# Two row transfers as one step of a planner, and a new rank table: a spectral filter and an MLP mixed by a gate, on one Trainium2 core

## The chip, the core and the metric

The kernel runs on one core of a Trainium2 chip. The core has TensorE (PE in the profile; its weight loads are PEld), VectorE (DVE), ScalarE (ACT), GpSimd (POOL), SyncE (SP, which here only issues transfers) and 16 DMA engines. Each engine works through its own instructions in the order in which the program holds them, and waits on semaphores for the others. The metric is the device time of one execution in microseconds (us), as the median of several runs; lower is better.

## The reference, cut to what matters

```python
def _A_ref(x, w_r, w_i):                      # x: 1 x 2048 x 512
    X = jnp.fft.rfft2(x, axes=(-2, -1))
    X = X * (w_r + 1j * w_i)                  # 2048 x 257
    return jnp.fft.irfft2(X, s=(S, D), axes=(-2, -1))

def _B_ref(x, w1, b1, w2, b2):
    h = jnp.einsum("bsd,df->bsf", x, w1) + b1   # F = 1792
    h = _gelu(h)
    return jnp.einsum("bsf,fd->bsd", h, w2) + b2

g = _sigmoid((x * gate_w).sum(-1, keepdims=True))
return g * a + (1 - g) * b                    # a = _A_ref, b = _B_ref, both of x
```

All data is float32. The output has 2048 x 512 elements.

## The kernel before, in words

**Arithmetic.** The MLP runs as matmuls on numbers that are split in a high part (rounded to 12 bits) and a low part: a product is three matmuls, high by high, high by low and low by high. Splitting costs one copy on ACT (the high part, names ending in h) and one subtraction on DVE (the low part, ending in l). The 2048 rows of x are four column blocks c of 512. F is 14 blocks f of 128. For blocks c = 0 and 1 (`mlp`, three passes over f) an up-projection is 12 matmuls into `ph`, then Gelu on ACT, then the split into `g_f h` and `g_f l` (L557, L558), then the down-projection in groups of three matmuls into `po`; ACT empties `po` into `o` (L1066, L1069) and a transfer adds it into `bacc` in HBM. Blocks 2 and 3 (`fast`, four passes) use a scheme with seven products for eight (`nu`, `ux`) and `poB`, `oB`.

**The spectral half.** The 2048 positions are 128 x 16. `forward(j)`, for 16 values of j, does the transform along the features (`pd`) and over 128 positions (`py`) by matmul and leaves the result in `y[j]`, a slice of one tile `yy` of 128 partitions; partition p below 64 holds the frequency p, partition 64 + p the frequency -p (partition 64: -64), each with real and imaginary part side by side. The transform over the remaining 16 values of j is two stages of four-point butterflies on DVE: `stage1` (tiles a0 to a3) and the first part of `filt` (b0 to b3), then the product with the filter (`wf` times `y` into `m`, L852, sums L854 and L856) and the way back: c0 to c3, `stage4` (d0 to d3) and `inverse` by matmul (`pz`, `pa`).

**The two special rows.** The frequencies p and -p are made as sum and difference of two rows; frequencies 0 and 64 have no such partner, so what rows 0 and 64 of `yy` get in this way is not their spectrum. `own_rows` (L738) computes these two rows by itself: eight small transfers (L732) gather them from all `y[j]` into a tile `own` of 64 partitions, one matmul with the constant `fx` does the 16-point transform (`pown`, L742), ACT copies the result to `ownr` (L744), and two transfers write it back, 32 partitions of `ownr` each into one partition of `yy` (L746). They overwrite what `stage1` left in those rows, so they come after all of `stage1`, and they come ahead of every instruction of `filt`, which reads whole tiles.

**The order.** Nothing is issued where it is written. The code makes 2017 steps; a step (`Graph.add`, L267) has an engine, a cost, a lag until its result is there, a function that emits its instructions, and the buffers that it reads and writes. From the buffers the graph takes what a step must wait for: the last writer of what it reads, and the last writer and all readers of what it writes. `schedule` (L309) then plays the steps through by their costs: whenever an engine is free it takes, among the steps whose predecessors are done and for which buffer slots are free, the one with the lowest rank (L326). For a transfer on SP a step is done at the end of its time on the wire plus its lag (L385), and only then do its successors become free. What comes out is one list of all steps, and the program is emitted in that order. The ranks come from the table `RANKS` (L128), one number for each step in the order of their making, times 0.05 (L1320). The numbers run from 0 to 2015 and come close to the step's place in the list.

So two things differ: in the planner the second transfer of L746 has the first as its predecessor (both write all of `Y`) and starts when that has landed by the planner's costs; in the emitted program each is an instruction of SP that waits for what it really depends on, and SP issues in the list's order.

What the steps are called that stand around these transfers:

- `gt` (L1285): four transfers that spread the gate's values over the partitions; `wf` (L843): one filter slice each; `wb9l_raw`, `wa11l_raw` and so on (L964): weights; `bacc<-o` (L1067): a down-projection's result to HBM.
- `g_8l`, `g_9l`, `g_5l` ... (L558): low parts of the hidden values for the down-projection, on DVE; the up-projection's accumulator `ph` is free only when the low part has been made.
- the product on `wf` with `rev` (L847): a few elements of a filter slice, on DVE.
- `b0d` (L754) and `b0s` (L752): the first two differences and sums of `filt(0)`.
- `xf`, `xft`, `tt`, `xb`: differences of x that `spread_x` (L1105) makes for blocks 2 and 3.

Of the kernel before, what the change touches and what calls it, by code (L numbers as in the profile page):

```python
# [37 lines left out]
HP = P // 2  # L38
# [394 lines left out]
def tile_kernel(ctx: ExitStack, tc: tile.TileContext, xt, xc, w1, w2, b1, b2, x0g, wf, wrev, out, consts):  # L433
# [10 lines left out]
    vec, act, pe, sp = nc.vector, nc.scalar, nc.tensor, nc.sync  # L444
# [9 lines left out]
    add = g.add  # L454
# [283 lines left out]
    def own_rows():  # L738
# [6 lines left out]
        for k in range(2):  # L745
            add("sp", 0.2, 2.6, lambda k=k: sp.dma_start(yy.ap()[k * HP:k * HP + 1], r.ap()[k * R // 2:(k + 1) * R // 2, 0]), [r], Y)  # L746
# [627 lines left out]
```

## Time and profile before

| | us |
|---|---|
| median of 3 runs | 368.69 (367.57 to 368.77) |
| the profiled execution's own time | 368.5 |
| its span, first to last instruction | 366.7 |
| PE busy in the span | 359.2 |
| DVE busy | 329.1 |
| ACT busy | 255.6 |
| POOL busy | 69.5 |

The span is 1.8 us shorter than the execution's own time: that is what lies around the instructions. The granted clock of TensorE is 0.999 over the whole span. A row of the profile's tables names a line, an engine, an operation and the tiles (out<-in, without numbers of buffers); "q" behind an engine is its issuing of transfers, which isn't counted as busy. Times of matmuls are modelled at their ends, and they overlap: a matmul of 512 columns is shown with 0.39 us and the next one starts 0.23 us after it.

### The profile page before, as it was taken

To read this page: it belongs to the slowest core of one execution; us is meant where nothing else is said; L and a number is where in the kernel's file an instruction comes from. 1 tells how busy PE (TensorE), PEld (TensorE's weight loads), DVE (VectorE), ACT (ScalarE), POOL (GpSimd) and SP (SyncE) were. 2 spreads that over 40 slices of the span, in tenths; PEclk is the share of its full clock that TensorE was granted. 3 is DMA by queue.
4 is the path that set the end of the run, shared out by engine and by line. 5 is a ranking of instruction groups with operands and counts; after the bars stand their busy time and mean duration, and the time that the engine had idled before them with its cause. 6 is when DMAs were issued, how large, how long until landed. Compare 5 with 4: busy or idle time off the path is not lost.

```text
span 366.7 us, 5738 instructions
## 1 busy us (share of the span) xinstructions
PE 359.2 (98%) x1808; PEld 302.8 (83%) x1808; DVE 329.1 (90%) x746; ACT 255.6 (70%) x471; POOL 69.5 (19%) x89
## 2 busy tenths in 40 slices
PE   8999999999999999999899999999999999999996
PEld 8888888898788778887688888888888788888885
DVE  5899989999838899999999999999999868989982
ACT  5976788788977222653758876999999997755300
POOL 0210001100204111220333200001241212112210
PEclk9999999999999999999999999999999999999999
DMA  7999785458787936999998954148788637899787
GB/s 250 284 336 309 240 250 132 88 170 252 185 196 133 215 39 123 314 203 337 210 236 200 209 133 117 57 150 207 118 146 170 94 53 157 171 296 230 190 254 217
DMA packets 46719, 70.35 MB, mean 192 GB/s; under 512 B 5600, under 2 KB 19424, under 8 KB 46688
## 3 DMA queue, kind: packets, MB, share of 16 engines
q1 hardware_dynamic: 34880, 48.93, 40.7%
q0 software_dynamic: 11376, 20.71, 35.5%
q8 instruction: 14, 0.23, 0.3%
q10 hardware_dynamic: 432, 0.33, 0.3%
q14 instruction: 17, 0.14, 0.1%
HBM read 48.32 MB, written 19.41 MB: 185 GB/s over the span
## 4 chain that ended last, share of the span: by engine, by line
PE 76%; DVE 12%; DMA 5%; ACT 3%; issue 2%; SPq 1%; DVEq 0%; ACTq 0%
PE poB L507 20%; PE po L507 13%; PE ph L507 12%; PE ux L1181 10%; PE nu L1181 8%; PE pz L507 4%; PE pd L507 3%; PE py L507 3%; PE pa L507 3%; DMA y<-ownr 2%; DVE m L852 2%; DMA wf<-in_wf 1%; DMA rev<-in_wrev 1%; DVE y L752 1%; DMA xf<-in_x0g 1%
## 5 line engine op out<-in xcount | busy, mean ns | idle before, releaser
L991 ACT ACTIVATE ph<-ph,b1t 128x512 f32<-128x512 f32 x28 | 18.4, 656 | 19.4 <-PE ph L507 19.3
L498 POOL DMA_DIRECT2D bacc<-o x16 | 14.3, 893 | 51.2 <-ACT o L1069 49.2
L890 ACT ACTIVATE sw<-y,al 64x512 f32<-64x512 f32 x32 | 22.5, 719 | 0.5
L498 POOL DMA_DIRECT2D bacc<-oB x16 | 14.3, 933 | 41.8 <-ACT oB L1069 41.6
L852 DVE TENSOR_TENSOR m<-y,wf 128x514 f32<-128x514 f32 x32 | 20.8, 690 | 0.0
L1069 ACT ACTIVATE o<-po 128x512 f32<-128x512 f32 x16 | 9.5, 595 | 15.8 <-PE po L507 15.8
L507 PE MATMUL pd<-cf,w 128*128 128x129 f32 x128 | 18.2, 275 | 0.2 <-DVE cf L622 0.2
L507 PEld LDWEIGHTS pz<-tg,pq 128*128 128x128 f32 x128 | 16.9, 191 | 1.5 <-ACT od L931 0.4
L507 PEld LDWEIGHTS pd<-cf,w 128*128 128x128 f32 x128 | 16.8, 190 | 1.3 <-DVE cf L622 0.4
L507 PE MATMUL pz<-tg,pq 128*128 128x128 f32 x128 | 17.4, 275 | 0.0
L1181 PE MATMUL nu<-xf,wa0h 128*128 128x512 f32 x56 | 17.4, 391 | 0.0
L507 PE MATMUL py<-zb,tf 128*128 128x258 f32 x96 | 17.2, 295 | 0.0
L897 DVE SCALAR_TENSOR_TENSOR pq<-y,al,sw 128x256 f32<-128x256 f32 x32 | 15.0, 480 | 0.7 <-ACT sw L893 0.7
L507 PEld LDWEIGHTS py<-zb,tf 128*128 128x128 f32 x96 | 14.1, 189 | 1.1 <-ACT pys L716 0.2
L507 PEld LDWEIGHTS pa<-zb,ci 128*128 128x128 f32 x96 | 13.8, 188 | 1.4
L507 PE MATMUL pa<-zb,ci 128*128 128x256 f32 x96 | 14.6, 283 | 0.0
L698 DVE TENSOR_TENSOR zb<-pd,zb 128x256 fp32r<-128x256 f32 x32 | 13.1, 418 | 0.9 <-ACT zb L695 0.7
L723 ACT ACTIVATE y<-pys 64x257 f32<-64x257 f32 x32 | 12.9, 416 | 1.3 <-DVE pys L720 0.8
L665 DVE TENSOR_TENSOR w<-eo 128x256 f32<-128x256 f32 x32 | 12.8, 418 | 0.0
L662 DVE TENSOR_TENSOR eo<-xf 128x256 f32<-128x256 f32 x32 | 12.6, 419 | 0.0
L910 DVE TENSOR_TENSOR zb<-pz,zb 128x512 fp32r<-128x512 f32 x16 | 11.0, 687 | 1.3 <-ACT zb L909 1.2
L1181 PEld LDWEIGHTS nu<-xf,wa0h 128*128 128x128 f32 x56 | 10.4, 188 | 2.1
(701 smaller groups left out, 1274.1 us busy)
## 6 DMA issues: line engine op xcount, KB each, us to landing
wf<-in_wf SPq DMA_DIRECT2D x16, 257.0 KB, 5.1
bacc<-o POOLq DMA_DIRECT2D x16, 256.0 KB, 5.9
bacc<-oB POOLq DMA_DIRECT2D x16, 256.0 KB, 4.5
xf<-in_xt SPq DMA_DIRECT2D x14, 256.0 KB, 5.2
wr<-in_w SPq DMA_DIRECT2D x14, 256.0 KB, 5.6
tf<-tf SPq DMA_DIRECT2D x16, 192.0 KB, 3.2
bacc<-o SPq DMA_DIRECT2D x8, 256.0 KB, 3.6
ba<-bacc SPq DMA_DIRECT2D x8, 256.0 KB, 4.5
```

The costliest lines, as they stand in the source:

```text
L498: return add("pool", 2.3 * kb / 340, 3.4, lambda: nc.gpsimd.dma_start(dst(), src(), accum_op=ALU.add), reads, writes, rank)
L507: pe.matmul(ps, w, x, start=start, stop=stop)
L662: v(lambda s=s, op=op: vec.tensor_tensor(eo.ap()[:, s], x.ap()[:, 0:2], x.ap()[:, 2:4], op=op), 256, [x], [(eo, s)], feed)
L665: v(lambda s=s, op=op: vec.tensor_tensor(w.ap()[:, s], eo.ap()[:, :, 0], eo.ap()[:, :, 1], op=op), 256, [eo], [(w, s)], feed)
L698: v(lambda c=c: vec.tensor_tensor(segs(xl, c), both(c), segs(xh, c), op=ALU.subtract), 256, [ps[c], (xh, c)], [(xl, c)], 0)
L723: a(lambda o=o, i=i: act.activation(Y[j].ap()[o:o + HP, 1], pys.ap()[i:i + HP, 1], AF.Copy), 257, [(pys, 1)], [(Y[j], 1 + k)], 0, more=0.1)
L852: v(lambda mk=mk, k=k, y=y, w=w: vec.tensor_tensor(mk.ap(), y.ap(), w.ap()[:, k:k + 1, :ND].to_broadcast([P, 2, ND]), op=ALU.mult), 514, [ ...
L890: a(lambda sw=sw, y=y, o=o, i=i: act.activation(sw.ap()[o:o + HP], y.ap()[i:i + HP, ::-1, :HD], AF.Copy, scale=al.ap()[i:i + HP, 0:1]), 51 ...
L897: v(lambda sw=sw, pq_=pq_, y=y, j=j, k=k, op=op: vec.scalar_tensor_tensor(pq_.ap()[:, k], y.ap()[:, k, :HD], al.ap()[:, 1 + j:2 + j], sw.a ...
L910: v(lambda n=n, ps=ps: vec.tensor_tensor(zl.ap()[:, :, :, n], ps.ap(), zh.ap()[:, :, :, n], op=ALU.subtract), 512, [ps, (zh, n)], [(zl, n) ...
L991: a(lambda: act.activation(ps.ap(), ps.ap(), AF.Gelu_apprx_tanh, bias=b1t.ap()[:, f:f + 1]), 600, [b1t], [ps]).table = "gelu"
L1181: pe.matmul(o.ap(), w(wi, e), FX[j].ap()[:, xi, e], start=first, stop=k == 5, skip_group_check=not start)
```

## The change

The two transfers of `own_rows` become one step that issues both; its cost is 0.4 instead of twice 0.2, its lag 3.0 instead of 2.6. There are 2016 steps then. The table of ranks is another one. Both kernels issue the same transfers and compute the same. The description of the change also says that a reader of one tile row no longer holds up the other's writer; no other line differs.

```diff
 RANKS = """
-11 19 10 20 28 24 44 42 36 41 34 7 14 0 13 16 21 4 43 32 12 8 5 3 6 9 120 60 74 83 85 39 52 67 96 17 22 26 95 97 109
...
+0 12 294 321 326 399 330 333 323 340 343 1 13 7 14 20 23 11 35 26 10 2 5 8 19 4 32 56 47 53 78 22 42 73 43 45 21 25 72
...
@@ -742,8 +742,12 @@
         add("pe", c_pe4(ND), 0.25, lambda: mm(ps.ap()[:, :ND], t.ap(), own.ap()[:, :ND], True, True), [t, own], [ps], 0)
         r = t2k("ownr", cls="own")
         a(lambda: act.activation(r.ap()[:R, 0], ps.ap()[:, :ND], AF.Copy), 257, [ps], [r], 0)
-        for k in range(2):
-            add("sp", 0.2, 2.6, lambda k=k: sp.dma_start(yy.ap()[k * HP:k * HP + 1], r.ap()[k * R // 2:(k + 1) * R // 2, 0]), [r], Y)
+
+        def back():
+            for k in range(2):
+                sp.dma_start(yy.ap()[k * HP:k * HP + 1], r.ap()[k * R // 2:(k + 1) * R // 2, 0])
+
+        add("sp", 0.4, 3.0, back, [r], Y)
```

The table holds one number for each step and can't be read as it stands. These are the ranks, old and new, of the steps around the transfers, found by counting the steps in the order of their making:

| step | engine | old rank | new rank |
|---|---|---|---|
| `bacc<-o` of block 1, last quarter | SP | 708 | 678 |
| `wb9l_raw` | SP | 711 | 693 |
| third `gt` | SP | 701 | 705 |
| `wf` of k2 = 8 | SP | 702 | 708 |
| `pown` | PE | 697 | 701 |
| `ownr` | ACT | 704 | 709 |
| last two differences of `stage1(3)` | DVE | 692, 696 | 702, 706 |
| the two row transfers | SP | 706, 719 | 712 (one step) |
| fourth `gt` | SP | 715 | 716 |
| `g_8l`, `g_9l` of block 0 | DVE | 710, 718 | 710, 722 |
| product on `wf` of k2 = 8 | DVE | 720 | 725 |
| first `b0d` | DVE | 734 | 726 |
| `g_5l` of block 1 | DVE | 725 | 730 |
| up-projections f = 5, 6, 7 of block 1 | PE | 713, 722, 730 | 714, 741, 732 |
| `sw3`, first half | ACT | 1422 | 1538 |
| first `d0s` | DVE | 1606 | 1532 |

154 rows, old and new, of the table RANKS are left out of this document.

## The prediction

> **What bounds the kernel now.** First the page's span and its row of busy times, to see which engine is full.
>
> ```profile
> span 366.7 us, 5738 instructions
> PE 359.2 (98%) x1808; PEld 302.8 (83%) x1808; DVE 329.1 (90%) x746; ACT 255.6 (70%) x471; POOL 69.5 (19%) x89
> ```
>
> TensorE (PE) is busy for 359.2 of 366.7 us, so nearly everything that can be won is time in which PE does not get its next matmul. Where that is, the view by stretches of time tells. Its columns are the stretch, its length, then busy us and instructions of PE, its weight loads, DVE, ACT and POOL, the granted clock, the share of the DMA engines and GB/s.
>
> ```profile
> 0.00:100.00 100.00, 98.25 (x552) 85.62 (x552) 89.77 (x243) 78.70 (x167) 11.88 (x23) 1.00 0.78 228
> 100.00:111.00 11.00, 11.00 (x49) 8.79 (x49) 4.08 (x9) 9.10 (x15) 1.72 (x2) 1.00 0.86 208
> 111.00:190.00 79.00, 77.39 (x336) 62.40 (x335) 76.71 (x162) 38.14 (x68) 20.13 (x23) 1.00 0.85 199
> 190.00:240.00 50.00, 50.00 (x222) 41.32 (x222) 48.92 (x101) 41.45 (x75) 7.86 (x9) 1.00 0.61 147
> 240.00:300.00 60.00, 59.48 (x308) 50.06 (x307) 56.15 (x118) 58.58 (x102) 14.91 (x18) 1.00 0.69 136
> 300.00:360.00 60.00, 60.00 (x325) 51.81 (x324) 51.80 (x112) 29.66 (x50) 12.99 (x15) 1.00 0.85 211
> 360.00:366.70 6.70, 3.08 (x25) 2.84 (x24) 1.66 (x5) 0.00 (x0) 0.00 (x0) 0.92 0.65 207
> ```
>
> From 111 to 190 us PE is idle for 1.6 us and DVE is at 76.71 of 79.00 us (97%). The matmuls overlap in their records, so the idle time understates the loss; the counts tell it. From 190 to 240 us PE has no idle time and runs 222 matmuls, one each 0.227 us (222 x 0.227 = 50.3 us, the last one hanging over the edge). At that pace the 336 of the stretch before need 76.2 us; with the same overhang that stretch had room for 79.3. So **PE loses about 3.1 us between 111 and 190 us**, and that is the largest loss inside the run (0 to 100 us: 1.75 us idle, 240 to 300 us: 0.52; the end, 3.6 us, is the last output's way home).
>
> Why DVE is late there, the chain of waits shows (start, length, what):
>
> ```profile
> 104.17 6.69 DMA y<-ownr
> 110.95 1.30 DVE b0d L754 x2
> ...
> 181.51 0.61 DVE g_12l L558
> 182.16 1.90 PE po L507 x7
> ```
>
> The chain runs from the second of the two row transfers (y<-ownr) into the first addition of the filter's first group (b0d) and through DVE to 182 us, where it passes to PE. DVE itself, in order of time:
>
> ```profile
> 101.20 0.69 DVE L754 TENSOR_TENSOR y<-a3s,a3s 128x514 f32<-128x514 f32 x1
> 102.79 0.69 DVE L558 TENSOR_TENSOR g_8l<-ph,g_8h 128x512 fp32r<-128x512 f32 x1 [0.91 <-ACT g_8h L557]
> 105.67 0.69 DVE L558 TENSOR_TENSOR g_9l<-ph,g_9h 128x512 fp32r<-128x512 f32 x1 [2.19 <-ACT g_9h L557]
> 106.28 0.16 DVE L847 SCALAR_TENSOR_TENSOR wf<-wf,rev 128x4 f32<-128x4 f32 x1
> 108.39 0.69 DVE L558 TENSOR_TENSOR g_5l<-ph,g_5h 128x512 fp32r<-128x512 f32 x1 [1.96 <-ACT g_5h L557]
> 110.95 1.30 DVE L754 TENSOR_TENSOR b0d<-y 128x514 f32<-128x514 f32 x2 [1.87 <-DMA y<-ownr]
> ```
>
> Between 101.89 and 110.95 us DVE does 2.2 us of small work (0.69 three times and 0.16) and stands for the other 6.8 us. The view charges only the last 1.87 us to the transfer, since the other gaps end with ACT; but those low parts are all that the order had left to run, and the filter, which then fills DVE up to 182 us, waits for the transfer the whole time. PE does not notice at once (11.00 of 11.00 us up to 111): it has matmuls of the second column block. It pays later, when DVE's backlog makes the low parts late.
>
> **The change part by part.** (1) *The two transfers go out back to back.* Before, SyncE issues them with three other steps between:
>
> ```profile
> 100.67 0.62 SPq L843 DMA_DIRECT2D wf<-in_wf  x1
> 101.97 0.59 SPq L746 DMA_DIRECT2D y<-ownr  x1
> 102.65 0.53 SPq L1067 DMA_DIRECT2D bacc<-o  x1
> 103.22 0.43 SPq L964 DMA_DIRECT2D wb9l_raw<-in_w  x1
> 103.70 0.43 SPq L1285 DMA_DIRECT2D gt<-gsc  x1
> 104.17 0.53 SPq L746 DMA_DIRECT2D y<-ownr  x1
> ```
>
> The second has no wait of its own on the chip (it starts 0.04 us after the issue before it); only the written order holds it, since the planner lets its step start when the first has landed. Three transfers of 256 KB lie ahead of it in SyncE's queue. The first one, with one such transfer ahead (wf), took
>
> ```profile
> DMA to landing us min/median/max: 3.1/3.1/3.1
> ```
>
> and the second 6.69 us. As one step, the pair costs the same two issues (0.59 and 0.53 us), so the second leaves some 0.6 us after the first and nothing is added on SyncE. In the new rank table two of the three steps that stood between (bacc<-o, wb9l_raw) go ahead of the pair and one (gt) behind it, which is then 0.5 us later. The matmul of the rows stands behind one more group of three matmuls (3 x 0.227 = 0.7 us), and the ACT copy that feeds the transfers behind ACT's high part g_8h (0.6 us, part of it beside the matmul); the last of DVE's first-stage sums, which the transfers overwrite and so wait for, is where it was. So I put the first issue at 102.7 instead of 101.97 and the second at 103.3. Ahead of it lie again three transfers of 256 KB (bacc<-o, wb9l_raw, wf), but issued 1 to 3 us before and not 0.5 to 1.5, so its way lies between 3.1 and 6.69 us; I take 4.0, nearer to the first, and get a landing at **107.3**. Bounds: 105.6 (issued as early as the first is now, 3.1 us) and 110.0 (103.3 and 6.69 us again).
>
> The Trainium skill speaks against so large a step: "DMA: Bandwidth & Descriptors", section "Anatomy of one DMA", gives a transfer a fixed cost of about 2.0 us plus its bytes at 436 GB/s (fitted on GpSimd's path; these go by SyncE's), an estimate of 2.1 us for 32 KB whatever is queued. By that the second would have landed at 106.3 already, which is the third rival below in the skill's own figure; the trace does not agree, with 6.69 us for one and 3.1 us for the other of two equal transfers.
>
> (2) *What DVE does with it.* In the new table the low part g_9l and the edge product of wf stay ahead of b0d and g_5l goes behind it. g_9l and the product end at 106.4, so b0d follows the landing, at 107.4 instead of 110.95: 3.55 us earlier, and with 0.6 us for g_5l now behind it DVE is **2.95 us ahead** (bounds: 0.25 from 110.0; 3.85 from 105.6, where b0d waits for the product). The same is seen in PE's order: two up-projections of 12 matmuls stood ahead of b0d that now stand behind (24 x 0.227 = 5.4 us of PE work).
>
> (3) *What PE makes of it.* PE can get back no more than the 3.1 us. The waits in that stretch (who <- whom: us, times, longest):
>
> ```profile
> ACT xft L1077 <- DVE tt L1081: 1.1, 1, 1.1
> PE po L507 <- ACT o L1069: 1.1, 1, 1.1
> PEld ph L507 <- DVE g_8l L558: 0.7, 1, 0.7
> PEld ph L507 <- DVE g_6l L558: 0.6, 1, 0.6
> PEld po L507 <- DVE g_12l L558: 0.5, 1, 0.5
> PEld ph L507 <- DVE g_11l L558: 0.5, 1, 0.5
> ```
>
> All go back to DVE; the largest by way of ACT, which takes its work in order: its copy of a difference (xft) waited for DVE (tt), and behind it stood the emptying of the accumulator (o) for which PE waited:
>
> ```profile
> 175.23 1.15 ACT L1077 ACTIVATE xft<-tt 128x512 fp32r<-128x512 f32 x2 [1.08 <-DVE tt L1081]
> 176.29 0.64 ACT L991 ACTIVATE ph<-ph,b1t 128x512 f32<-128x512 f32 x1
> 176.86 0.59 ACT L1069 ACTIVATE o<-po 128x512 f32<-128x512 f32 x1
> ```
>
> With DVE 2.95 us ahead, g_12l ends at 179.15 instead of 182.1; PE without loss would ask for it at about 182.1 - 3.0 = 179.1. So the lead is just enough and not ample. I leave three waits of some 0.25 us, as the small ones above are, and take 3.1 - 0.75 = **2.3 us won**; the bounds are nothing (lead 0.25) and 3.1.
>
> (4) *The order made anew.* Every rank changes, mostly by a few places; the instructions stay the same. For 0 to 100 us and 240 to 300 us I take no difference: what PE loses there (0.7 us inside the first, without its first 1.06 us, and 0.52) is a dozen small waits that a new order deals afresh. From 111 to 190 us 1.6 us idle stood for 3.1 lost; in that proportion these 1.2 us are an estimated 2.4, which can go or double. As deviation I take 1.2 each way.
>
> Sum: 2.3 us from the profiled execution's 368.5 gives 366.2; the median of the runs shown, 368.69, lies 0.2 above it, so **366.4**.
>
> **The rivals.** *The lead is spent (no change).* DVE is 97% full from 111 to 190 us; the new table also moves filter work ahead of low parts (g_6l and g_7l of the second column block now stand behind several more of the filter's products), so the low parts may come as late as now. Or the pair lands late (110.0), DVE is 0.25 us ahead, and PE wins that at best. Against it: the lead is DVE time that stood idle, and the work is the same. Time 367.6 to 369.0, about 368.3.
>
> *A new wait in ACT's stage (slower).* From 240 to 300 us ACT is at 58.58 of 60.00 us, and there the new table moves most: a copy of the inverse part (sw3) from rank 1422 to 1538, a sum (d0s0) from 1606 to 1532. ACT works in order; one copy placed ahead of the DVE result that it needs holds up every emptying of an accumulator behind it, and PE stands as it did once for 1.1 us (the rows above). With the 2.3 us won it needs more than three such waits (2.3 + 1.1 = 3.4 us) to come out slower by over 1.1 us: four give 366.4 + 4.4 = 370.8, less the 0.5 us that the stage loses now, 370.3. For it: ACT has 1.4 us of slack in 60. Against it: PE stood only 0.52 us there under the old order.
>
> *A transfer of this size always takes 3.1 us, and the stall is not the queue's (no change).* Then the second landed at 107.3 already, something else held b0d until 110.95, and the change moves the second landing by 104.17 - 103.3 = 0.9 us, of which g_5l's 0.6 us is lost again: 368.4. Against it stands the row of the chain that ends the 6.69 us at b0d.
>
> **How the numbers follow.** 0.3% of 368.69, or 1.1 us, is about what a measurement of this kernel can tell from no change. The forecast (366.4, own range 364.9 to 367.5) gets 0.58, the lead spent 0.24, the 3.1 us rule 0.04, ACT's stage 0.14. Faster by over 0.3% 0.58, within it 0.28, slower 0.14. The range goes from all 3.1 us won with 0.9 from the new order (368.7 - 4.0 = 364.7) to the upper end of the cases without change, 369.1; what it leaves out is nearly all of the slower rival and little below.
>
> **What would show it.** Right: in the timeline two issues of y<-ownr in a row, the second landing within 5 us; b0d's start at 106.4 to 108 us; DVE's idle time from 102 us to b0d down from 6.8 to some 4 us; at least 10 more matmuls in the 79 us behind b0d's old start; g_12l ending before 180 us. Wrong in step 1: a way of over 6 us. Wrong in step 3: b0d early, yet the same count of matmuls. Wrong in step 4: the stretches 0 to 100 or 240 to 300 us with over 1 us more or less PE idle time than now; then the sum is off by what the new order dealt.

## The result and the profile after

| | before | after |
|---|---|---|
| median of 8 runs each (us) | 368.47 | 365.98 |
| lowest to highest (us) | 367.44 to 369.49 | 364.86 to 368.04 |
| ratio, 95% interval | 1 | 0.9938 [0.991, 0.9965] |
| profiled execution, its span (us) | 368.50, 366.7 | 368.04, 366.2 |

The changed kernel is faster by 0.35 to 0.9%, at 366.0 us against the 366.4 forecast. The execution of it that was profiled is the slowest of its eight, so a second one was taken later, of the same kernel unchanged (label e0_new_again, 366.34 us); both are read here, and each profile row below comes from one execution. All lines behind the transfers stand four lines lower than in the kernel before.

First the page of the profiled execution, span and busy times:

```profile
span 366.2 us, 5746 instructions
PE 358.7 (98%) x1808; PEld 302.9 (83%) x1808; DVE 327.8 (90%) x746; ACT 256.7 (70%) x471; POOL 69.6 (19%) x89
```

Then its view by stretches (stretch, length, then busy us and instructions of PE, weight loads, DVE, ACT and POOL, clock, DMA share, GB/s):

```profile
0.00:100.00 100.00, 98.29 (x550) 85.58 (x551) 87.51 (x241) 79.19 (x168) 11.87 (x23) 1.00 0.79 228
111.00:190.00 79.00, 78.12 (x343) 63.68 (x342) 77.38 (x163) 39.31 (x69) 20.27 (x23) 1.00 0.87 199
240.00:300.00 60.00, 59.77 (x315) 50.77 (x314) 53.29 (x112) 58.89 (x103) 15.71 (x18) 1.00 0.70 137
```

and one of them from the second execution:

```profile
111.00:190.00 79.00, 78.23 (x345) 64.40 (x344) 76.28 (x162) 39.86 (x70) 20.27 (x23) 1.00 0.87 197
```

Before, PE ran 336 matmuls from 111 to 190 us; now 343 and 345. At 0.227 us each that is 1.6 and 2.0 us of the 3.1 us that were lost there. The medians moved by 2.5 us (368.47 to 365.98) and, for the second set of runs of the same kernel, by 2.1 us (368.65 to 366.59); what the part above 2.0 us comes from is not shown. Below, "PE's loss" of any kernel means this: 3.1 us less 0.227 us for each matmul over 336.

What set it off is seen on SyncE's queue in the first execution (order of time: start, length, what):

```profile
101.75 0.63 SPq L847 DMA_DIRECT2D wf<-in_wf  x1
103.77 1.22 SPq L748 DMA_DIRECT2D y<-ownr  x2
```

and on its DVE (the idle time before an instruction, and what ended it, in brackets):

```profile
103.01 0.69 DVE L758 TENSOR_TENSOR y<-a3d,a3d 128x514 f32<-128x514 f32 x1
109.40 1.30 DVE L758 TENSOR_TENSOR b0d<-y 128x514 f32<-128x514 f32 x2 [2.56 <-DMA y<-ownr]
180.16 0.69 DVE L558 TENSOR_TENSOR g_12l<-ph,g_12h 128x512 fp32r<-128x512 f32 x1
```

The same two views of the second execution, SyncE's queue:

```profile
102.44 1.22 SPq L748 DMA_DIRECT2D y<-ownr  x2
```

and DVE:

```profile
106.43 1.29 DVE L758 TENSOR_TENSOR b0d<-y 128x514 f32<-128x514 f32 x2
```

The issues are one group (x2). In the first execution DVE's last first-stage sum ends at 103.70 us and the pair, which waits for it, leaves at 103.77 us. The chain of waits of that execution has the second transfer's way, its time from issue to landing:

```profile
104.42 4.89 DMA y<-ownr
```

In the second execution the view of the transfers gives both ways:

```profile
DMA to landing us min/median/max: 3.2/3.4/3.5
```

Nothing on DVE waited for them there. b0d starts 1.55 and 4.52 us earlier than the 110.95 us of before.

### The profile page after: what moved, and what is told of

Same layout as the page of the kernel before. It is cut to its first block, busy times and chain, and to the rows that moved or that the text cites. A ratio compares the mean times of both kernels' runs of the same rounds, so it can differ in the third digit from the quotient of the medians.

```text
span 366.2 us, 5746 instructions
## 1 busy us (share of the span) xinstructions
PE 358.7 (98%) x1808; PEld 302.9 (83%) x1808; DVE 327.8 (90%) x746; ACT 256.7 (70%) x471; POOL 69.6 (19%) x89
## 4 chain that ended last, share of the span: by engine, by line
PE 75%; DVE 12%; DMA 5%; ACT 4%; issue 2%; SPq 1%; DVEq 0%; ACTq 0%
PE poB L507 20%; PE po L507 13%; PE ph L507 11%; PE ux L1185 9%; PE nu L1185 7%; PE pd L507 4%; PE pz L507 3%; PE py L507 3%; PE pa L507 3%; DVE m L856 3%; DMA wf<-in_wf 3%; DMA y<-ownr 1%; DMA xf<-in_xt 1%; DVE y L760 1%; DVE y L758 1%
## 5 line engine op out<-in xcount | busy, mean ns | idle before, releaser
L498 POOL DMA_DIRECT2D bacc<-o x16 | 15.3, 1029 | 43.2 <-ACT o L1073 43.2
L695 ACT ACTIVATE zb<-pd 128x256 fp32r<-128x256 f32 x32 | 11.6, 384 | 3.9 <-PE py L507 3.9
L698 DVE TENSOR_TENSOR zb<-pd,zb 128x256 fp32r<-128x256 f32 x32 | 12.5, 417 | 1.1 <-ACT zb L695 1.1
```

The lines of the kernel that those rows point to most:

```text
L498: return add("pool", 2.3 * kb / 340, 3.4, lambda: nc.gpsimd.dma_start(dst(), src(), accum_op=ALU.add), reads, writes, rank)
L695: a(lambda c=c: act.activation(segs(xh, c), both(c), AF.Copy), 256, [ps[c]], [(xh, c)], 0)
L698: v(lambda c=c: vec.tensor_tensor(segs(xl, c), both(c), segs(xh, c), op=ALU.subtract), 256, [ps[c], (xh, c)], [(xl, c)], 0)
```

## The experiments

Two theories stood at the start. L: the second transfer lands earlier, DVE gets a lead (it starts the filter earlier), PE takes it back between 111 and 190 us. N: the new ranks as a whole order the work better, and the pair is incidental. The runs of before beside the experiments have medians of 368.65 us (29 runs), 368.44 (29) and 368.44 (35), one for each group of four kernels. Several edits move one step in the finished order with this helper, behind the planner's call:

```python
    def behind(n, m):
        order.remove(g.steps[n])
        order.insert(order.index(g.steps[m]) + 1, g.steps[n])
```

**The changed kernel again, the pair alone, and the new order without the early second transfer.**

> The changed kernel once more, unchanged, for the spread of its profile beside the others on this chip. Both theories: ratio about 0.994. Theory L: PE loses some 1.7 us between 111 and 190 us where the old order lost 3.1, and b0d starts near 109 us; the end behind the last matmul, 4.8 us in the first profile of this kernel and 3.6 in that of the old one, is nearer to 3.6.

> The old plan as it was, every instruction in its old place, except that the second row transfer is issued directly behind the first. DVE's order is the old one, so g_5l (end 109.1 us in the old profile) still stands ahead of b0d. Theory L (the earlier landing gives DVE a lead, and PE gets it back between 111 and 190 us): second landing some 105.5 to 107 us, b0d at 109.1 instead of 110.95, lead 1.85 us, of which PE gets 1 to 1.8: ratio 0.995 to 0.997. Theory N (the gain of the change comes from the new order elsewhere, the landing is hidden): b0d may start earlier, but the time is the old one, ratio 0.999 to 1.001.

```diff
--- before
+    behind(480, 479)
```

> The new order, with the second row transfer issued three places later, behind the fourth gt and wa11l_raw, as it stood behind three others in the old order. Theory L: it lands 1.5 to 3 us later, b0d at 111 to 112.5 instead of 109.4 us, and PE loses most of that again: ratio 0.998 to 1.001. Theory N: ratio as that of the change, 0.993 to 0.995.

```diff
--- after
-        def back():
-            for k in range(2):
-                sp.dma_start(yy.ap()[k * HP:k * HP + 1], r.ap()[k * R // 2:(k + 1) * R // 2, 0])
+        def back(k):
+            sp.dma_start(yy.ap()[k * HP:k * HP + 1], r.ap()[k * R // 2:(k + 1) * R // 2, 0])
 
-        add("sp", 0.4, 3.0, back, [r], Y)
+        add("sp", 0.4, 3.0, lambda: back(0), [r], Y).second = lambda: back(1)
...
             s.emit()
+            if s.n == 799:
+                g.steps[479].second()
```

Step 799 is the load of wa11l_raw, so the second transfer again leaves behind gt and that load. Measured, with the ratio to before and its 95% interval (here and below not exactly the quotient of the medians): the changed kernel (e0) 366.59 us, 0.9959 [0.9938, 0.998]; the pair in the old order (e1) 366.88, 0.9957 [0.9937, 0.9977]; the new order split (e3) 372.97, 1.0126 [1.0093, 1.0159]. Neither theory had expected the time of e3. The pair in the old order, SyncE's queue:

```profile
102.15 1.22 SPq L746 DMA_DIRECT2D y<-ownr  x2
```

its DVE:

```profile
108.87 1.29 DVE L754 TENSOR_TENSOR b0d<-y 128x514 f32<-128x514 f32 x2
```

and its stretch:

```profile
111.00:190.00 79.00, 78.45 (x345) 64.27 (x345) 76.77 (x162) 41.42 (x73) 21.26 (x25) 1.00 0.88 203
```

One moved issue gives the whole gain: 345 matmuls, as in the second execution of the changed kernel. The new order split, its DVE:

```profile
111.97 1.30 DVE L757 TENSOR_TENSOR b0d<-y 128x514 f32<-128x514 f32 x2 [5.21 <-DMA y<-ownr]
```

its stretch:

```profile
111.00:190.00 79.00, 74.44 (x318) 60.10 (x318) 73.58 (x154) 36.64 (x64) 17.82 (x21) 0.98 0.81 186
```

and the longest waits of PE in it (who <- whom: us, times, longest):

```profile
PE ph L507 <- DVE g_6l L558: 3.0, 1, 3.0
PE ph L507 <- DVE g_10l L558: 0.9, 1, 0.9
```

18 matmuls fewer than before, though b0d is only 1.0 us later: PE stands for low parts, 3.0 us for g_6l alone. DVE has this low part at

```profile
125.94 0.68 DVE L558 TENSOR_TENSOR g_6l<-ph,g_6h 128x512 fp32r<-128x512 f32 x1
```

which is 14.0 us behind b0d, as in the first execution of the changed kernel (109.40 to 123.36 us); in the old order it came 12.5 us behind (110.95 to 123.47). So the new order puts g_6l later behind b0d, and with b0d late too it is too late for PE. Not all of the loss is waiting: behind this wait the granted clock was 0.50 from 127 to 129 us. From 121 to 131 us PE ran 25 matmuls where 44 would fit, which is 4.3 of the 7.2 us lost. N falls in its plain form; L stands, with a correction: the new order does not merely use an early landing, it depends on one.

**The parts as the planner makes them.** The same question without a moved step: the merged step under the old ranks, and two steps under the new ones.

> The merged step of the changed kernel with the rank table of before (the second transfer's rank left out), the order planned again. Both transfers go out together, the rest is before's order as far as the planner keeps it. Theory L (the earlier landing gives DVE its lead, PE takes it back between 111 and 190 us): as the pair in the old order, 366.3 to 367.3, ratio 0.994 to 0.997, b0d at 106.5 to 109.5. Rival N (the gain needs the new ranks): 368.3 to 369.5, ratio 1.000 or a little over it. An earlier landing that is spent on a missing table of the filter (wf) or weight would be seen as a wait of DVE of over 1 us at 118 to 124 us.

> The two separate steps of before with the new ranks, the order planned again: the second transfer may start in the plan only when the first has landed. Theory L: the second goes out late, b0d starts at 111 us or later, and as in the new order with a late second transfer (372.97) the time is above before: 370 to 374, ratio 1.004 to 1.015. Rival N (the new ranks are good by themselves): 366 to 367.5, ratio below 0.997.

```diff
--- after, to e4
 RANKS = """
-0 12 294 321 326 399 330 333 323 340 343 1 13 7 14 20 23 11 35 26 10 2 5 8 19 4 32 56 47 53 78 22 42 73 43 45 21 25 72
+11 19 10 20 28 24 44 42 36 41 34 7 14 0 13 16 21 4 43 32 12 8 5 3 6 9 120 60 74 83 85 39 52 67 96 17 22 26 95 97 109
...
--- before, to e5
 RANKS = """
-11 19 10 20 28 24 44 42 36 41 34 7 14 0 13 16 21 4 43 32 12 8 5 3 6 9 120 60 74 83 85 39 52 67 96 17 22 26 95 97 109
+0 12 294 321 326 399 330 333 323 340 343 1 13 7 14 20 23 11 35 26 10 2 5 8 19 4 32 56 47 53 78 22 42 73 43 45 21 25 72
...
```

In e4 the old table lacks its entry for step 480; in e5 the new table has the pair's entry twice.

Measured: 368.01 us, 1.0007 [0.9986, 1.0029] (e4), and 375.42, 1.0214 [1.0189, 1.024] (e5). The second, e5, is slower, as L has it, and by more than was expected; its stretch:

```profile
111.00:190.00 79.00, 74.60 (x315) 60.54 (x314) 72.46 (x151) 35.26 (x63) 17.69 (x20) 0.96 0.78 188
```

and its DVE:

```profile
111.28 1.30 DVE L754 TENSOR_TENSOR b0d<-y 128x514 f32<-128x514 f32 x2 [2.22 <-DMA y<-ownr]
```

But PE's longest wait there is for a weight and not for a low part:

```profile
PE po L507 <- DMA wb10l<-in_w: 2.1, 1, 2.1
PE ph L507 <- DVE g_11l L558: 1.6, 1, 1.6
```

Behind these two waits the granted clock was 0.50 from 159 to 165 us. From 151 to 166 us PE ran 37 matmuls where 66 would fit, 6.6 of the 7.9 us lost in the stretch. How much of that goes back to the late landing, this run does not show; e3 is the clean test.

The first, e4, is a miss for L. Its pair lands early enough that b0d starts at 105.86 us, earliest of all, and PE runs 342 matmuls, but DVE spends the lead on the filter and does g_6l late, behind c0d:

```profile
105.86 1.29 DVE L758 TENSOR_TENSOR b0d<-y 128x514 f32<-128x514 f32 x2
122.59 1.29 DVE L758 TENSOR_TENSOR c0d<-y 128x512 f32<-128x512 f32 x2
123.79 0.68 DVE L558 TENSOR_TENSOR g_6l<-ph,g_6h 128x512 fp32r<-128x512 f32 x1
```

and PE, in order of time, waits for it:

```profile
124.53 0.50 PE L507 MATMUL ph<-mxh,wa8h 128*128 128x512 f32 x1 [0.99 <-DVE g_6l L558]
```

Ahead of c0d DVE also stands 0.37 and 1.22 us for a filter slice (wf, at 117.0 and 122.1 us); the expectation had named this sign. Behind the stretch PE idles again: 49.66 of 50.00 us busy from 190 to 240 us, with 219 matmuls where before had 222. That takes back 0.7 of the 1.4 us won in the stretch; where the rest goes is not shown. So a lead of 5 us at b0d is worth nothing in itself; what counts is when the low parts come. Once the filter may start early, the planner with the old ranks lets it pass them.

**More of a lead in the old order.**

> As e1, and on DVE the low part g_5l of block 1 goes behind the two differences b0d, as in the new order; all else in the old order. Theory L: b0d at 106.4 to 107.5 us, DVE some 3 us ahead, of which PE gets 1.8 to 2.8: ratio 0.992 to 0.995. Theory N: ratio 0.999 to 1.001, with b0d early all the same.

> The order of before with the pair together and g_5l behind b0d, and now the load of wb9l_raw ahead of the pair, as the new order has it. If the lead that b0d had there was lost because this weight was late for PE (the stall of 1.7 us at 116 us): the stall is gone, PE loses 1.2 us or less between 111 and 190 us, 366.3 to 367.0. If the lead is lost otherwise (DVE waits for the filter's table wf, or g_5l behind b0d makes the low parts late): 367.3 to 367.9 as without it. If the pair has to wait behind this load: b0d after 108.5 us.

```diff
--- before (both)
+    behind(480, 479)
+    behind(741, 907)
--- e11 alone
+    behind(702, 926)
```

Steps 741 and 907 are g_5l and the second b0d; 702 is the load of wb9l_raw, 926 that of wf ahead of the pair. Measured: 367.61 us, 0.9985 [0.9963, 1.0006] (e2, less than L expected), and 366.99, 0.9976 [0.9956, 0.9995] (e11). b0d starts at 107.61 and 107.44 us. In the first (e2) the load of wb9l_raw behind the pair took SyncE 2.23 us to issue (its queue):

```profile
104.67 2.23 SPq L964 DMA_DIRECT2D wb9l_raw<-in_w  x1
```

and PE stood for the weight made of it:

```profile
118.16 0.50 PE L507 MATMUL po<-g_9h,wb9l 128*128 128x512 f32 x1 [1.51 <-DMA wb9l<-in_w]
```

which its stretch shows as 337 matmuls:

```profile
111.00:190.00 79.00, 77.22 (x337) 62.63 (x337) 74.02 (x157) 40.52 (x70) 21.07 (x24) 1.00 0.87 208
```

With that load ahead of the pair (e11) the stall is gone:

```profile
111.00:190.00 79.00, 78.34 (x344) 64.07 (x343) 75.57 (x160) 39.61 (x71) 20.31 (x24) 1.00 0.91 206
```

The lead had been lost to a weight. The times of the two do not differ beyond their intervals, so this is shown in the stretch alone. And b0d 1.4 us earlier than with the pair alone (107.44 against 108.87 us), with g_5l's 0.6 us now behind it, buys nothing: 344 matmuls against 345.

**Is it SyncE's queue?** The prediction put the 6.69 us down to what lies ahead in that queue. Here the second transfer goes by ACT's own queue, at two places. The expectations call it theory Q that SyncE's queue makes the transfer slow.

> The kernel of before with the second transfer issued by ACT's own queue, in which no 256 KB transfer is queued, at the time at which SyncE issued it (about 104.2 us), nothing else moved. Theory Q (the 6.69 us come from the three 256 KB transfers ahead of it in SyncE's queue): it takes 2.5 to 4 us, lands at 107 to 108.3, b0d follows g_5l at 108.9, and the time is that of the pair in the old order, 366.5 to 367.3. Rival I (the engines that move the bytes are busy whatever the queue): 5 to 7 us, landing at 109.5 to 111.2, b0d at 110 to 111, time 368.0 to 369.0.

> The kernel of before with the second transfer issued by ACT's own queue behind ACT's high part g_9h, so not before 104.2 us, and nothing of 256 KB ahead of it in its own queue. Theory Q (what is queued ahead in SyncE's queue makes the 6.69 us): it takes 3 to 4.5 us, lands by 108.8, b0d at 108.9, 366.6 to 367.2. Rival I (from 104 us on the transfer is slow in any queue, because of the bytes that all queues move then): 6 to 7.2 us, b0d at 110.5 to 111.5, 368 to 369.

```diff
--- before (both)
-        for k in range(2):
-            add("sp", 0.2, 2.6, lambda k=k: sp.dma_start(...), [r], Y)
+        for k in range(2):
+            add("sp", 0.2, 2.6, lambda k=k: (sp, act)[k].dma_start(...), [r], Y)
--- e8 alone
+    s = g.steps[480]
+    acts = [x for x in order[:order.index(s)] if x.eng == "act"]
+    order.remove(s)
+    order.insert(order.index(acts[-2]), s)
```

Measured: 366.97 us, 0.9968 [0.9952, 0.9985] (e8), and 368.38, 0.9995 [0.9971, 1.0018] (e12). The first missed its purpose. Its issue stands in ACT's list behind a copy that starts at 103.19 us, yet ACT's queue has it at once, with the first one:

```profile
102.42 0.62 ACTq L746 DMA_DIRECT2D y<-ownr  x1
```

and the view of the transfers gives the two ways:

```profile
DMA to landing us min/median/max: 4.3/4.4/4.5
```

So it is another form of the pair (345 matmuls), with ways no shorter than in one queue. The second (e12) went late:

```profile
105.63 0.61 ACTq L746 DMA_DIRECT2D y<-ownr  x1
```

with these ways, the last its own:

```profile
DMA to landing us min/median/max: 3.6/4.9/6.1
```

and DVE behind it:

```profile
111.87 1.30 DVE L754 TENSOR_TENSOR b0d<-y 128x514 f32<-128x514 f32 x2 [2.27 <-DMA y<-ownr]
```

With nothing of 256 KB ahead of it in its own queue it took 6.1 us, b0d waited, and PE ran 337 matmuls: the kernel of before again (the traced execution took 369.26 us). Q falls, as far as one execution can tell: the transfer was slow with no bulk ahead of it in its own queue.

**Two mends of the changed kernel.** PE has two stalls of its own in it, one at the start and one at 163 us (PE in order of time, first execution):

```profile
10.50 0.74 PE L507 MATMUL ph<-mxh,wa1h 128*128 128x256 f32 x4 [0.64 <-ACT mxh L650]
164.66 0.50 PE L507 MATMUL ph<-mxh,wa12h 128*128 128x512 f32 x1 [0.51 <-DVE g_10l L558]
```

> The changed kernel with one load moved: the first raw low weight (wb0l_raw) goes to SyncE's queue behind the two input tiles (xf8, xf12) and not ahead of them, as before had it. The stall of 0.7 to 0.8 us that PE has at 9.6 us in the changed kernel, in ph for the high part that ACT makes of these tiles, should go. If that time comes through to the end: 365.8 to 366.2, ratio against before 0.9935. If it is absorbed by a later wait, or the weight is then late: 366.4 to 367.5.

> The changed kernel with the first raw low weight's load behind the two input tiles, and now also ACT's copy of it (wb0h) behind the two high parts (mxh) of these tiles, so that ACT waits for the inputs alone. The stall of 0.7 to 0.8 us that PE has at 9.6 us in the changed kernel should go, and PE's granted clock stays at 1.00 from 10 to 15 us. If it comes through to the end: 365.7 to 366.1, ratio against before about 0.993. If a later wait takes it: 366.4 to 366.9, ratio 0.995 to 0.996.

> The kernel with the mended start, and in DVE's list the low part g_10l of the second column block ahead of three products of the filter (3 of 0.6 us) and not behind them. PE's stall of 0.7 to 0.9 us at 163 us, between po of g_10h and ph of wa12h, which waits for this low part, should go; the three products come 0.6 us later. If DVE's order there is what holds PE: 0.6 to 0.9 us below the kernel with the mended start alone, 364.9 to 365.5. If PE only meets the next late low part: within 0.3 us of it.

```diff
--- after (all three)
+    behind(509, 16)
--- e9 and e10
+    behind(510, 118)
--- e10 alone
+    behind(866, 1011)
+    behind(867, 866)
+    behind(868, 867)
```

Steps 509 and 510 are the load of wb0l_raw and ACT's copy of it, 16 and 118 the load of xf12 and its high part; 866 to 868 make g_10l, 1011 is the sum ahead of the three products. Measured: 368.18 us, 0.9999 [0.9979, 1.0019] (e7); 366.53, 0.9959 [0.9939, 0.9979] (e9); 367.01, 0.9965 [0.9949, 0.998] (e10). The first (e7) made the start worse: ACT works in order, its copy of the weight still stood ahead of the high parts, and now the weight was the later of the two. ACT:

```profile
9.62 0.63 ACT L969 ACTIVATE wb0h<-wb0l_raw 128x512 fp32r<-128x512 f32 x1 [2.74 <-DMA wb0l_raw<-in_w]
```

PE:

```profile
11.34 0.91 PE L507 MATMUL ph<-mxh,wa1h 128*128 128x256 f32 x4 [1.81 <-ACT mxh L650]
```

and the stretch around it, with the granted clock at 0.67:

```profile
10.00:15.00 5.00, 3.66 (x18) 3.66 (x19) 4.20 (x13) 4.63 (x9) 2.41 (x3) 0.67 1.05 368
```

With the copy moved too (e9), the stall at 10 us is gone, but PE's waits from 12 to 52 us show two others:

```profile
PE po L507 <- DMA wb0l<-in_w: 0.8, 1, 0.8
PE ph L507 <- ACT o L1070: 0.7, 1, 0.7
```

and the time is that of the changed kernel (366.53 against 366.59). The third (e10) removes the stall at 163 us, and PE stands instead at another low part:

```profile
181.10 0.47 PE L507 MATMUL po<-g_10h,wb10h 128*128 128x512 f32 x1 [0.54 <-DVE g_12l L558]
```

No version here beats the changed kernel by more than the intervals.

All kernels beside each other (times and ratios as above):

| kernel | order | b0d at (us) | matmuls 111 to 190 | PE's loss (us) | ratio |
|---|---|---|---|---|---|
| before | old | 110.95 | 336 | 3.1 | 1 |
| e12, second late by ACT | old | 111.87 | 337 | 2.9 | 0.9995 |
| e1, pair | old | 108.87 | 345 | 1.1 | 0.9957 |
| e8, second at once by ACT | old | 108.54 | 345 | 1.1 | 0.9968 |
| e2, pair and b0d ahead | old | 107.61 | 337 | 2.9 | 0.9985 |
| e11, the same, weight ahead | old | 107.44 | 344 | 1.3 | 0.9976 |
| e4, merged step | old ranks, planned anew | 105.86 | 342 | 1.7 | 1.0007 |
| after (first execution) | new | 109.40 | 343 | 1.5 | 0.9938 |
| e0, after (second) | new | 106.43 | 345 | 1.1 | 0.9959 |
| e7, inputs first | new | 109.19 | 347 | 0.6 | 0.9999 |
| e9, start mended | new | 107.29 | 346 | 0.8 | 0.9959 |
| e10, and g_10l ahead | new | 107.81 | 346 | 0.8 | 0.9965 |
| e3, new order split | new | 111.97 | 318 | 7.2 | 1.0126 |
| e5, two steps | new ranks, planned anew | 111.28 | 315 | 7.9 | 1.0214 |

Each row is one profiled execution; the two of the changed kernel differ by 2 matmuls, or 0.5 us. The table reads as a step, not a slope. With b0d at 109.4 us or earlier, PE loses 0.6 to 1.7 us wherever b0d stands, unless a weight is late (e2); with b0d at 111 us or later it loses 3 us in the old order and 7 to 8 in the new one, part of that at half the clock and in e5 behind a late weight. No kernel has b0d between 109.4 and 110.9 us, so where the step lies is open.

## Why the prediction came out as it did

*The whole.* The mechanism named, the second transfer's landing, is the one that moved the time: taken alone it gives the gain (e1), taken away from the changed kernel the gain turns into a loss (e3; e5 too, but most of its loss stands behind a late weight).

*Step 1, the landing.* The pair left at 103.77 and 102.44 us (102.7 forecast), and the second transfer's way was 4.89 and at most 3.5 us (4.0 forecast). The statement that DVE's last first-stage sum is "where it was" did not hold in the first execution: it ended at 103.70 instead of 101.89 us, DVE having done 87.51 us of work in the first 100 instead of 89.77; in the second execution it was not late. The landing, 109.3 us there, stayed inside the bounds. What failed is the reason given for the size: "three transfers of 256 KB lie ahead of it in SyncE's queue". Put on a queue with no such load, the late transfer was about as slow, 6.1 us (e12). It did not spoil the number, since the same two issues also put the pair ahead of the burst of weight loads; that this came to about 4 us is luck as far as the queue was the reason.

*Step 2, DVE's lead.* Forecast 107.4 us for b0d; measured 109.40 and 106.43, on both sides of it.

*Step 3, what PE makes of it.* 2.3 us forecast, 1.6 and 2.0 measured, so the term was a little too large (222 x 0.227 is 50.4 and 336 x 0.227 is 76.3, each 0.1 more than was written; the 3.1 us stays); the mark of at least 10 more matmuls was missed by 3 and 1. g_12l was to end before 180 us; it ended at 180.8 us in the first execution and at 179.8 in the second. "The lead is just enough and not ample" was wrong: by the table b0d 1.5 us earlier does what b0d 4 us earlier does. And the rest of the loss is not three waits of 0.25 us: in the first execution its largest piece is the one at g_10l, 0.5 us, which when moved away turned up at g_12l (e10).

*Step 4, the new order.* Put at nothing, with 1.2 us either way, and the runs agree as far as they go: the changed kernel and the pair in the old order give 0.9959 and 0.9957. It is a balance, though. From 240 to 300 us PE idles 0.23 us instead of 0.52 and runs 7 matmuls more; at the end the last output's way home is longer, in the first execution 4.8 us from PE's end (361.5 us) to the span's (366.2), where before had 3.6 us and the second execution has 3.9. The prediction did not ask what the new ranks are for: under the planner the merged step alone gains nothing (e4).

*The rivals.* "The lead is spent" did not happen in the changed kernel, but it describes e4 and e2, in two forms: low parts passed by the filter, and a weight or filter slice that is late. The wait in ACT's stage did not come. "Always 3.1 us" is refuted by ways of 2.8 (e4) to 7.46 us (e3) for equal transfers. The Trainium skill's "DMA: Bandwidth & Descriptors", section "Anatomy of one DMA", fitted on GpSimd's path, gave an estimate of 2.1 us whatever is queued; the traces do not agree, the shortest of these ways is 0.7 us longer.

## What to carry to other kernels

Where the last transfer of a group releases a whole stage, try to issue the group back to back and ahead of the bulk loads; here a planner that let the second start only when the first had landed cost the time of what it put between. Once that transfer was early enough, more earliness was worth nothing: look at when the next small results come out of the engine that it releases. And when an order by priorities has adapted to a late event, an earlier event can need the priorities of the work that it competes with to be set anew, or the lead goes to the wrong work, as in e4.

## What had not been expected of the hardware

*A 32 KB transfer's way went with what had been asked for just before it.* Issued directly behind the first, with one 256 KB load from SyncE in the 2.1 us ahead of the pair, the second took at most 3.5 us (second execution after) and 4.89 us (first), and at most 4.1 us in the seven other kernels with the pair on SyncE, also in e7, where the pair left only at 104.67 us. Issued at 104.11 to 105.63 us with two or more such transfers from SyncE in the 1.5 us before, it took 6.69 (before), 7.46 (e3), 7.08 (e5) and, on a queue of its own, 6.1 us (e12). Bytes of all queues that meet on their way would explain it; that is argued, and the kept traces do not settle it: the DMA engines' mean busy share was 0.86 to 0.94 over the four slow ways and 0.69 to 0.88 over the others.

*One issue in such a burst takes long.* SyncE's issues of 256 KB around these transfers take 0.3 to 0.65 us, but in most runs one in the burst takes more: 1.50 us (wa12l_raw) in before, 2.40 (wa12l_raw) in the second execution after, 2.23 (wb9l_raw) in e2, 1.86 (gt) in e8; in e3 and e5 none did. In e2 the weight loaded by it was 1.5 us late for PE.

*PE's clock after a standstill.* In e7 PE stood 1.81 us before 11.34 us, and the granted clock from 10 to 15 us was 0.67; in e9, without that standstill, it was 1.00. In e3 it was 0.50 from 127 to 129 us behind the wait of 3.0 us, in e5 0.50 from 159 to 165 us behind the waits of 2.1 and 1.6 us. Behind shorter waits, 0.99 us in e4 and 1.51 us in e2, it stayed at 1.00 (121 to 126 us).

*A transfer left ahead of the arithmetic that stands before it.* In e8 the transfer on ACT's queue left at 102.42 us, while the copy directly before it in ACT's list started at 103.19.
